# Linear attention into a snake MLP on one core: weights by casting DMAs, filler products, paired PSUM tiles early, and the exponentials of two batches in a row

## The chip, the cores and the metric

The kernel runs on one NeuronCore of a Trainium2 chip. Time is device time in microseconds (us) of one launch on that core; the number that counts is the median of several runs. The engines are PE (TensorE, matrix products), DVE (VectorE), ACT (ScalarE), POOL (GpSimd) and SP (SyncE, which here only starts DMAs). PE's clock has two levels, shown as a granted share of 1.00 or 0.50.

## The reference, cut to what matters

```python
batch, n_heads, seq, head_dim = (8, 8, 576, 64)
n_tokens, d_model, d_ff = (4608, 512, 2048)
...
q_s = q - np.max(q, axis=-1, keepdims=True)
q_s = np.exp(q_s)
q_s = q_s / (np.sum(q_s, axis=-1, keepdims=True) + 1e-09)
k_s = k - np.max(k, axis=2, keepdims=True)
k_s = np.exp(k_s)
k_s = k_s / (np.sum(k_s, axis=2, keepdims=True) + 1e-09)
kv = np.einsum('bhsd,bhse->bhde', k_s, v)
return np.einsum('bhsd,bhde->bhse', q_s, kv).astype(np.float32)
...
x = np.ascontiguousarray(attn_out.transpose(0, 2, 1, 3)).reshape(B * S, H * D)
...
h = x @ w_in
s = np.sin(alpha * h)
g = h + s * s / (alpha + 1e-09)
return (g @ w_out).astype(np.float32)
```

All inputs and the output are float32 in the chip's memory. q, k and v have 9.4 MB each, w_in and w_out 4.19 MB each.

## The kernel before

The work has two halves. **Attention** goes batch by batch (8 of them, called 0 to 7). ACT takes the exponentials of q and k, two instructions each (`exp_q`, `exp_k`); `cast_v` brings v to bfloat16; `norm_q` divides q by its row sums on DVE and POOL. PE then forms k'v (`kv_mm`, 36 products), turns q over (`q_transpose`, 12 products and 6) and multiplies the two (`attn_out`, four groups of 4); between these, DVE or ACT copy each result out of PSUM. The result is `xT`, the tokens of the batch as columns.

The **MLP** goes in 9 tiles t of 512 tokens. For each of 16 slices ni of d_ff, PE makes h (`mm_h`, 4 products of 512 columns), ACT its sine, and then ACT, POOL or DVE squares it (the letter A, P or D of a string such as `SQ0`); DVE adds it up into g (`combine`). Then PE multiplies g by w_out, 64 products of 512 columns for the tile's four groups j of 128 tokens (`mm_o`), and a copy (`evac_o`) goes out by DMA. In this text h(t) and o(t) are these two stages of tile t. Tile t needs batches up to t, so the attention of batch t + 1 is woven into the stages of tile t: the generators `o_pair` and `o_stream` hand out the products of o(t), and `take(os, n)` places n of them between the steps of the attention.

The order on every engine is the order in which the code is written (`tc.manual_schedule()`). Waits come from the buffers: tiles are taken from pools in turn, and a new one waits until the last reader of the buffer is done. PSUM has 8 banks: four for h (`ps_h`), two for o (`ps_o`) and one buffer of two banks for the attention (`ps_a`).

All loads stand on SP's queue, in this order: alpha, q, k and v of batch 0, the four parts of w_in, the four of w_out, then batches 1 and 2. All go through one pool of six float32 buffers (`stage`). The weights are brought to bfloat16 by POOL: w_in part 0 before h(0) starts, the others between the squares of h(0), the last part of w_out after it.

From tile 3 on, the exponentials of batch t + 1 stand behind slice 0 of h(t) (`attn_front`), its matrix products in h(t) (`attn_back`), and o(t - 1) is woven through. Before that, the code is written out: batch 1 in o(0), batch 2 in o(1), batch 3 in h(2), whose slice 2 is followed by the exponentials of batch 3 and by the rest of o(1):

```python
if ni == 2:
    flush(lag, 0)
    attn_front(3, [GP])
    take(os)
attn_back(3, ni - 7)
```

At the start, PE makes 14 products without use (`warm`) while batch 0 is prepared.

Of the kernel before, what the change touches and what calls it, by code (L numbers as in the profile page):

```python
# [23 lines left out]
def kernel(  # L24
# [247 lines left out]

    def cast_win(c, eng, parts=1):
        n = 4 // parts
        for h in range(parts):
            eng(win[:, h * n:(h + 1) * n, c * 512:(c + 1) * 512], wst["i", c][:, h * n:(h + 1) * n])

    def cast_wout(c, eng):
        eng(wout[:, 4 * c:4 * c + 4, :], wst["o", c])  # L279
# [202 lines left out]
```

## Time and profile before

| | |
|---|---|
| median of 3 runs | 320.58 us (320.1 to 322.48) |
| profiled execution, its own time | 321.48 us |
| its span, first to last instruction | 319.7 us |
| PE busy | 290.9 us, 91% of the span |
| ACT, DVE, POOL busy | 231.8, 197.6, 82.8 us |
| mean granted clock of PE | 0.984 |
| DMA, from 3 us to 52 us | about 390 GB/s without a break |

The profiled execution took 1.78 us more than its span, and 0.90 us more than the median. PE is the engine to look at: where it is idle, or at the lower clock, the row just before says what it waited for. From 119 us on the kernel repeats itself every 31.7 us.

### The profile page before, as it was taken

How to read it: one execution, taken by the hardware profiler on the slowest of the kernel's cores; microseconds unless marked ns; L12 is line 12 of the kernel's file. 1: busy time of each engine (PE TensorE's matmuls, PEld its weight loads, DVE VectorE, ACT ScalarE, POOL GpSimd, SP SyncE). 2: the span in 40 equal slices, each digit the busy share in tenths (PEclk: the TensorE clock that was granted, in tenths of full speed). 3: DMA queues.
4: the chain of work that ended last, by engine and by line, in shares of the span. 5: the costliest groups of instructions: out<-in, count | busy, mean ns of one | idle time of the engine just before them, and what ended most of it. 6: DMA issues, size and time to landing. Idle time of an engine off the chain costs nothing.

```text
span 319.7 us, 4552 instructions
## 1 busy us (share of the span) xinstructions
PE 290.9 (91%) x1727; PEld 133.9 (42%) x1727; DVE 197.6 (62%) x281; ACT 231.8 (72%) x321; POOL 82.8 (26%) x58
## 2 busy tenths in 40 slices
PE   2889897999795969999999999999999999999994
PEld 1434343444341524544454445444544444444441
DVE  2738982498535784687568756875687545455511
ACT  4759852997099659976997799779977777777600
POOL 0439970474245550700061007000400000000000
PEclk9959999999998999999999999999999999999999
DMA  7999996780279900111861186111111121111142
GB/s 254 384 387 386 391 391 257 202 309 0 66 225 310 397 23 0 35 36 33 259 252 33 36 264 246 33 33 36 33 35 33 33 56 45 33 33 36 34 98 66
DMA packets 22790, 46.44 MB, mean 145 GB/s; under 512 B 1760, under 2 KB 1776, under 8 KB 22768
## 3 DMA queue, kind: packets, MB, share of 16 engines
q1 hardware_dynamic: 22688, 46.02, 43.9%
q8 instruction: 13, 0.21, 0.3%
q10 hardware_dynamic: 80, 0.13, 0.1%
q14 instruction: 9, 0.07, 0.1%
HBM read 36.71 MB, written 9.44 MB: 144 GB/s over the span
## 4 chain that ended last, share of the span: by engine, by line
PE 54%; ACT 19%; DVE 13%; POOL 7%; issue 4%; DMA 1%; SPq 0%; ACTq 0%; POOLq 0%; DVEq 0%
PE hp L215 23%; PE op L235 23%; DVE g L231 6%; ACT s L221 5%; POOL s L225 3%; ACT qe L119 3%; ACT ke L119 3%; PE tp L185 3%; DVE qs L147 2%; ACT L119 2%; ACT L221 2%; PE xp L198 2%; PE kvp L158 2%; ACT s L223 2%; POOL wout L279 2%
## 5 line engine op out<-in xcount | busy, mean ns | idle before, releaser
L215 PE MATMUL hp<-xT,win 128*128 128x512 bf16 x544 | 140.0, 387 | 8.7 <-DVE g L231 5.9
L231 DVE SCALAR_TENSOR_TENSOR g<-s,inva_sb,hp 128x512 bf16<-128x512 f32 x136 | 100.2, 745 | 70.3 <-ACT s L223 56.1
L235 PE MATMUL op<-wout,g 128*128 128x512 bf16 x544 | 135.5, 379 | 1.7 <-DVE o L244 0.8
L221 ACT ACTIVATE s<-hp,alpha_sb 128x512 f32<-128x512 f32 x136 | 92.2, 683 | 39.2 <-PE hp L215 35.0
L215 PEld LDWEIGHTS <-win 128*128 128x128 bf16 x576 | 56.6, 99 | 79.7 <-issue 16.1
L235 PEld LDWEIGHTS <-g 128*128 128x128 bf16 x576 | 53.5, 98 | 64.6 <-issue 2.3
L223 ACT ACTIVATE s<-s 128x512 f32<-128x512 f32 x115 | 72.4, 630 | 3.7
L149 POOL TENSOR_TENSOR qn<-qe,qs 128x2304 bf16<-128x2304 bf16 (+1 forms) x8 | 26.6, 3328 | 95.3 <-PE hp L215 80.6
L225 POOL TENSOR_TENSOR s<-s 128x512 f32<-128x512 f32 x22 | 25.0, 1144 | 38.4 <-ACT s L221 38.3
L147 DVE TENSOR_REDUCE qs<-qe 128x18 f32<-128x1152 bf16 (+1 forms) x11 | 20.8, 1887 | 17.2 <-ACT qe L119 17.2
L244 DVE COPY o<-op 128x512 f32<-128x512 f32 x32 | 21.5, 674 | 7.1 <-PE op L235 7.1
L201 DVE CAST xT<-xp 128x512 bf16<-128x512 f32 (+1 forms) x26 | 19.1, 739 | 4.4 <-PE xp L198 4.4
L119 ACT ACTIVATE qe<-st_q 128x1152 bf16<-128x1152 f32 x16 | 17.8, 1156 | 4.1 <-DMA st_q<-in_q_dram 4.1
L119 ACT ACTIVATE ke<-st_k 128x1152 bf16<-128x1152 f32 x16 | 17.7, 1150 | 0.7 <-DMA st_k<-in_k_dram 0.7
L133 POOL CAST vb<-st_v 128x1152 bf16<-128x1152 f32 x13 | 15.9, 1252 | 4.2 <-DMA st_v<-in_v_dram 4.2
L201 ACT CAST xT<-xp 128x640 bf16<-128x640 f32 x6 | 4.0, 690 | 15.4 <-PE xp L198 15.4
L198 PE MATMUL xp<-qT,kvb 64*64 64x256 bf16 (+1 forms) x128 | 9.8, 302 | 4.0 <-DVE xT L201 1.2
L185 PE MATMUL tp<-identb,qn 128*128 128x128 bf16 x144 | 10.8, 219 | 3.0 <-ACT qT L186 1.1
L185 PEld LDWEIGHTS <-qn 128*128 128x128 bf16 x144 | 9.1, 98 | 7.6 <-issue 3.9
L198 PEld LDWEIGHTS <-kvb 64*64 64x64 bf16 x128 | 4.7, 103 | 15.8 <-issue 13.9
L158 PE MATMUL kvp<-vb,ke 64*128 64x130 bf16 x288 | 10.3, 223 | 0.7 <-ACT qT L186 0.5
L119 ACT ACT_TABLE_LOAD x8 | 10.3, 1283 | 0.9 <-PEq L466 0.7
(38 smaller groups left out, 113.2 us busy)
## 6 DMA issues: line engine op xcount, KB each, us to landing
out_dram<-o SPq DMA_DIRECT2D x71, 128.0 KB, 2.4
st_q<-in_q_dram SPq DMA_DIRECT2D x7, 1152.0 KB, 5.9
st_k<-in_k_dram SPq DMA_DIRECT2D x7, 1152.0 KB, 8.4
...
st_w<-in_moe_w_out_dram SPq DMA_DIRECT2D x4, 1024.0 KB, 15.4
...
```

The source lines that it names most:

```text
L119: nc.scalar.activation(dst[:, :, ii * 128:(ii + 1) * 128].rearrange("p j (x d) -> p x j d", x=2), src[:, ii::2], AX.Exp)
L147: nc.vector.tensor_reduce(part, src, axis=AXL.X, op=ALU.add)
L149: engs[h].tensor_tensor(dst, src, part.unsqueeze(3).to_broadcast([128, J, w, D]), op=ALU.mult)
L185: nc.tensor.transpose(tp[:, h, 2 * jj + ii], qn[:, j, ii * 128:(ii + 1) * 128], identb)
L201: eng(xT[:, ii::2, c0:c0 + n], xp[:, :, 0:n])
L215: nc.tensor.matmul(hp, win[:, ki, ni * 128:(ni + 1) * 128], xT[:, ki, t * MF:(t + 1) * MF], start=(ki == 0), stop=(ki == 3))
L221: nc.scalar.activation(s, hp, AX.Sin, scale=alpha_sb[:, ni:ni + 1])
L223: nc.scalar.activation(s, s, AX.Square)
L225: nc.gpsimd.tensor_tensor(s, s, s, op=ALU.mult)
L231: nc.vector.scalar_tensor_tensor(G[t][:, ni], in0=s, scalar=inva_sb[:, ni:ni + 1], in1=hp, op0=ALU.mult, op1=ALU.add)
L235: nc.tensor.matmul(acc, G[t][:, ni, j * 128:(j + 1) * 128], wout[:, ni, :], start=(ni == 0), stop=(ni == nN - 1))
L244: eng(o, acc)
```

## The change

The weights no longer pass through float32 buffers and POOL's casts: eight DMAs on POOL's own queue write w_in and w_out to their bfloat16 places, and they stand behind POOL's half of `norm_q(0)`. Batch 1 is loaded from POOL's queue too, after slices 4, 7 and 10 of h(0), and batch 2 after `cast_v(1)`; q and k of batch 3 are loaded before h(1), v of batch 3 after the exponentials of batch 3. `stage` has five buffers in place of six. alpha is loaded by ACT's queue, not ahead of q on SP's.

Four products without use stand before `attn_out` of batch 0 and four behind it. Up to the end of h(1) the four banks of `ps_o` and `ps_a` are one pool of two buffers with two banks each (`ps_e`): a pair of h slices, a pair of o groups, or a step of the attention. h(0) uses the string of h(1), with nine squares on POOL. `qe` has two buffers, and the exponentials of batch 3 follow those of batch 2 on ACT, ahead of o(1); the copies of o(1) stand on ACT behind them. The rest of o(1) is spread over h(2), one product for each slice. A sine of one element (`zero`) loads ACT's table ahead of h(1) and of h(2).

```diff
-    stage = ctx.enter_context(tc.tile_pool(name="stage", bufs=6))
+    stage = ctx.enter_context(tc.tile_pool(name="stage", bufs=5))
...
-    def load(name, t, b, halves=False):
+    def load(name, t, b, halves=False, eng=nc.sync):
...
             for ii in range(2):
-                nc.sync.dma_start(out=flat[:, ii::2], in_=view[:, ii::2])
+                eng.dma_start(out=flat[:, ii::2], in_=view[:, ii::2])
         else:
-            nc.sync.dma_start(out=flat, in_=view)
+            eng.dma_start(out=flat, in_=view)
...
-    wst = {}
-
-    def load_win(c, parts=1):
-        st = stage.tile([128, 4, 512], F32, name="st_w", tag="st")
-        n = 4 // parts
-        for h in range(parts):
-            nc.sync.dma_start(out=st[:, h * n:(h + 1) * n], in_=win_v[:, h * n:(h + 1) * n, c * 512:(c + 1) * 512])
-        wst["i", c] = st
+    def load_win(c):
+        nc.gpsimd.dma_start(out=win[:, :, c * 512:(c + 1) * 512], in_=win_v[:, :, c * 512:(c + 1) * 512])
 
     def load_wout(c):
-        st = stage.tile([128, 4, 512], F32, name="st_w", tag="st")
-        nc.sync.dma_start(out=st, in_=wout_v[:, 4 * c:4 * c + 4, :])
-        wst["o", c] = st
+        nc.gpsimd.dma_start(out=wout[:, 4 * c:4 * c + 4, :], in_=wout_v[:, 4 * c:4 * c + 4, :])
...
     def exp_q(b):
-        A["qe", b] = att1.tile([128, J, 4 * D], BF16, name="qe")
+        A["qe", b] = att2.tile([128, J, 4 * D], BF16, name="qe")
...
         if wide and ni % 6 >= 4:
-            hp = ps_o.tile([128, MF], F32, name="op", tag="o")
+            if ni % 6 == 4:
+                A["hh"] = wide.tile([128, 2, MF], F32, name="hh", tag="a")
+            hp = A["hh"][:, ni % 6 - 4]
         else:
             hp = ps_h.tile([128, MF], F32, name="hp", tag="h")
...
-    nc.sync.dma_start(out=alpha_rows, in_=moe_alpha.rearrange("(no ni) -> no ni", ni=128))
+    nc.scalar.dma_start(out=alpha_rows, in_=moe_alpha.rearrange("(no ni) -> no ni", ni=128))
...
-    load_win(0, parts=2)
-    for c in range(1, 4):
-        load_win(c)
-    for c in range(4):
-        load_wout(c)
-    load("q", q, 1)
-    load("k", k, 1)
-    load("v", v, 1, halves=True)
-    load_batch(2)
...
-        for n in range(14):
-            nc.tensor.matmul(warm, identb, A["qe", 0][:, 0:4, 0:128], start=True, stop=True)
+
+        def warm_up(n):
+            for _ in range(n):
+                nc.tensor.matmul(warm, identb, A["qe", 0][:, 0:4, 0:128], start=True, stop=True)
+
+        warm_up(14)
         norm_q(0, [GP, V])
+        for c in range(4):
+            load_win(c)
+        for c in range(4):
+            load_wout(c)
         cast_v(0, [V, V])
...
         kv_norm(0)
-        cast_win(0, POOL_CP, parts=2)
+        warm_up(4)
         for ii in range(2):
             attn_out(0, ii, 0, ps_s, DVE_CP)
             attn_out(0, ii, 1, ps_s, ACT_CP)
+        warm_up(4)
...
-    ps_o = ctx.enter_context(tc.tile_pool(name="ps_o", bufs=2, space=PSUM, reuse_waits="tile"))
-    ps_a = ctx.enter_context(tc.tile_pool(name="ps_a", bufs=1, space=PSUM, reuse_waits="tile"))
...
-    lag = []
-    SQ0 = "ADPADPADPADPADPA"
-    for ni in range(nN):
-        h_slot(0, ni, SQ0[ni], lag, wide=True)
-        flush(lag, 1)
-        if ni in (0, 2, 5):
-            cast_win((0, 2, 5).index(ni) + 1, POOL_CP)
-        elif ni in (8, 11, 14):
-            cast_wout((8, 11, 14).index(ni), POOL_CP)
-    flush(lag, 0)
-    cast_wout(3, POOL_CP)
...
         for n in range(2):
-            evac_o(t, j0 + n, accs[n], (DVE_CP, ACT_CP)[n])
-            if n == 0:
-                yield
...
+            evac_o(t, j0 + n, accs[n], engs[n])
+        yield
...
-    exp_q(1)
-    norm_q(1, [GP, V])
-    os = o_pair(0, 0, ps_o)
-    take(os)
-    exp_k(1)
-    cast_v(1, [GP, V])
-    os = o_pair(0, 2, ps_h)
-    take(os, 16)
-    q_transpose(1, 0, ps_a, ACT_CP)
-    take(os, 2)
-    q_transpose(1, 1, ps_a, ACT_CP)
-    take(os, 2)
-    kv_mm(1, 0, ps_a)
-    kv_mm(1, 1, ps_a)
-    kv_norm(1)
-    take(os, 6)
-    for ii in range(2):
-        attn_out(1, ii, 0, ps_a, DVE_CP)
...
+    lag = []
+    SQ = "PAPDPAPAPPDPAPAP"
+    with tc.tile_pool(name="ps_e", bufs=2, space=PSUM, reuse_waits="tile") as ps_e:
+        late = {4: ("q", q, 1, False), 7: ("k", k, 1, False), 10: ("v", v, 1, True)}
+        for ni in range(nN):
+            h_slot(0, ni, SQ[ni], lag, ps_e)
+            flush(lag, 1)
+            if ni in late:
+                name, x, b, hv = late[ni]
+                load(name, x, b, halves=hv, eng=GP)
+        flush(lag, 0)
+
+        exp_q(1)
+        norm_q(1, [GP, V])
+        acc = ps_e.tile([128, 2, dm], F32, name="acc", tag="a")
+        take(o_pair(0, 0, [acc[:, 0], acc[:, 1]], [ACT_CP, ACT_CP]))
+        exp_k(1)
+        cast_v(1, [GP, V])
+        for name, x in (("q", q), ("k", k), ("v", v)):
+            load(name, x, 2, eng=GP)
+        os = o_pair(0, 2, [ps_h.tile([128, dm], F32, name="hp", tag="h") for _ in range(2)], [DVE_CP, ACT_CP])
+        take(os, 18)
+        q_transpose(1, 0, ps_e, ACT_CP)
+        nc.scalar.activation(zero, zero, AX.Sin)
         take(os, 2)
-        attn_out(1, ii, 1, ps_a, ACT_CP)
-        take(os, 1)
-    take(os)
-
-    SQ1 = "PAPDPAPAPPDPAPAP"
-    for ni in range(nN):
-        h_slot(1, ni, SQ1[ni], lag, wide=True)
-        flush(lag, 1)
-    flush(lag, 0)
...
+        q_transpose(1, 1, ps_e, DVE_CP)
+        take(os, 2)
+        kv_mm(1, 0, ps_e)
+        kv_mm(1, 1, ps_e)
+        kv_norm(1)
+        take(os, 6)
+        for ii in range(2):
+            attn_out(1, ii, 0, ps_e, DVE_CP)
+            attn_out(1, ii, 1, ps_e, ACT_CP)
+            take(os, 2)
+        take(os)
+        load("q", q, 3)
+        load("k", k, 3)
+
+        for ni in range(nN):
+            h_slot(1, ni, SQ[ni], lag, ps_e)
+            flush(lag, 1)
+            if ni == 14:
+                cast_v(2, [GP, GP])
+        flush(lag, 0)
+
+    ps_o = ctx.enter_context(tc.tile_pool(name="ps_o", bufs=2, space=PSUM, reuse_waits="tile"))
+    ps_a = ctx.enter_context(tc.tile_pool(name="ps_a", bufs=1, space=PSUM, reuse_waits="tile"))
...
+    def o_stream(t, eng=DVE_CP):
...
                 if ni == nN - 1:
-                    evac_o(t, j, acc, DVE_CP, last=(t == nT - 1 and j == 3))
+                    evac_o(t, j, acc, eng, last=(t == nT - 1 and j == 3))
...
-    def attn_front(b, engs):
-        exp_q(b)
-        exp_k(b)
-        cast_v(b, [GP, GP])
-        norm_q(b, engs)
-        if b + 1 < B:
-            load_batch(b + 1)
-
-
-    attn_front(2, [V, GP])
-    os = o_stream(1)
+
+    exp_q(2)
+    exp_k(2)
+    norm_q(2, [V, GP])
+    exp_q(3)
+    exp_k(3)
+    load("v", v, 3)
+    cast_v(3, [GP, GP])
+    nc.scalar.activation(zero, zero, AX.Sin)
+    os = o_stream(1, ACT_CP)
     take(os, 32)
...
-    take(os, 4)
+    take(os, 3)
...
+    norm_q(3, [GP])
     for n in range(4):
-        attn_out(2, n // 2, n % 2, ps_a, (DVE_CP, ACT_CP)[n % 2])
-        take(os, 2)
+        attn_out(2, n // 2, n % 2, ps_a, ACT_CP)
+        take(os, 3)
+    load_batch(4)
...
     for ni in range(nN):
-        hp = h_slot(2, ni, SQ2[ni], lag)
+        h_slot(2, ni, SQ2[ni], lag)
         flush(lag, 1)
-        if ni == 2:
-            flush(lag, 0)
-            attn_front(3, [GP])
-            take(os)
-        attn_back(3, ni - 7)
+        attn_back(3, ni - 6)
+        take(os, 1)
     flush(lag, 0)
+    take(os)
```

On POOL's queue, from its half of the division of q of batch 0 (`qn`) into h(0), before (`st_w` is a float32 buffer of a weight part, L225 a square):

```order
L149 TENSOR_TENSOR qn<-qe,qs 128x9x128
L276 CAST win<-st_w 128x2x512 x2
L276 CAST win<-st_w 128x4x512
L225 TENSOR_TENSOR s<-s 128x512
L276 CAST win<-st_w 128x4x512
L225 TENSOR_TENSOR s<-s 128x512
L276 CAST win<-st_w 128x4x512
L225 TENSOR_TENSOR s<-s 128x512
L279 CAST wout<-st_w 128x2048
```

The same place of POOL's queue in the changed kernel, up to that step of batch 1:

```order
L141 TENSOR_TENSOR qn<-qe,qs 128x9x128
L101 DMA win<-in_moe_w_in_dram 128x4x512 x4
L104 DMA wout<-in_moe_w_out_dram 128x4x512 x4
L219 TENSOR_TENSOR s<-s 128x512 x3
L92 DMA st_q<-in_q_dram 128x4x576
L219 TENSOR_TENSOR s<-s 128x512
L92 DMA st_k<-in_k_dram 128x4x576
L219 TENSOR_TENSOR s<-s 128x512 x2
L90 DMA st_v<-in_v_dram 128x2x576 x2
L219 TENSOR_TENSOR s<-s 128x512 x3
L141 TENSOR_TENSOR qn<-qe,qs 128x9x128
```

Over the whole stretch up to that step of batch 1, nine casts are gone, twelve DMAs have come in, and there are nine squares in place of five.

On ACT's queue, from the last sine of h(1) on, before (`xT` is a copy of the attention of batch 2, L221 a sine of h(2), L223 a square):

```order
L221 ACTIVATE s_761<-hp_756,alpha_sb_87 128x512
L119 ACT_TABLE_LOAD
L119 ACTIVATE qe_766<-st_q_125 128x2x9x64 x2
L119 ACTIVATE ke_769<-st_k_127 128x2x9x64 x2
L201 CAST xT_83<-xp_914 128x2x320
L201 CAST xT_83<-xp_934 128x2x320
L221 ACT_TABLE_LOAD
L221 ACTIVATE s_949<-hp_944,alpha_sb_87 128x512
L221 ACTIVATE s_957<-hp_952,alpha_sb_87 128x512
L223 ACTIVATE s_957<-s_957 128x512
L221 ACTIVATE s_966<-hp_961,alpha_sb_87 128x512
L119 ACT_TABLE_LOAD
```

The exponentials of batch 3 (`qe_971`, `ke_974`) and a second table load follow there. The same place of ACT's queue in the changed kernel (`o<-op` is a copy of a group of o(1)):

```order
L215 ACTIVATE s_750<-hp_745,alpha_sb_87 128x512
L111 ACT_TABLE_LOAD
L111 ACTIVATE qe_762<-st_q_468 128x2x9x64 x2
L111 ACTIVATE ke_765<-st_k_470 128x2x9x64 x2
L111 ACTIVATE qe_776<-st_q_606 128x2x9x64 x2
L111 ACTIVATE ke_779<-st_k_608 128x2x9x64 x2
L384 ACT_TABLE_LOAD
L384 ACTIVATE zero_106<-zero_106 128x1
L238 COPY o_804<-op_787 128x512
L238 COPY o_825<-op_808 128x512
L193 CAST xT_83<-xp_909 128x2x256
```

The exponentials of batch 3 have moved out of h(2) to those of batch 2, one pair of table loads is gone, and the copies of o(1) stand behind all of it.

## Rows read from the trace of the kernel before

**Rows 1.** Windows by stage: h(0) start, attention 1, o(1), h(2) twice, steady tile.

```profile
core 0: us, PE busy (x) PEld busy (x) DVE busy (x) ACT busy (x) POOL busy (x), PEclk, DMA share, GB/s
17.30:23.70 6.40, 6.38 (x17) 2.23 (x17) 2.01 (x3) 2.70 (x4) 2.19 (x2) 0.53 1.05 386
...
46.20:56.50 10.30, 7.76 (x88) 4.11 (x87) 3.38 (x7) 3.01 (x4) 0.00 (x0) 1.00 0.72 265
...
72.40:92.00 19.60, 16.82 (x128) 7.85 (x126) 11.54 (x18) 9.70 (x12) 6.05 (x5) 1.00 0.21 46
92.00:103.00 11.00, 7.11 (x32) 3.00 (x30) 6.38 (x7) 10.88 (x13) 6.86 (x5) 0.94 0.97 339
103.00:119.00 16.00, 12.93 (x107) 6.47 (x106) 12.81 (x21) 9.93 (x16) 8.67 (x9) 0.93 0.59 220
...
151.00:182.70 31.70, 31.33 (x199) 14.51 (x198) 22.01 (x32) 27.30 (x38) 6.32 (x3) 1.00 0.45 146
```

**Rows 2.** Timeline, 0 to 30 us: start, us, engine, line, op, tiles, count.

```profile
1.20 0.92 SPq L90 DMA_DIRECT2D st_q<-in_q_dram  x2
...
8.22 2.13 POOL L149 TENSOR_TENSOR qn<-qe,qs 128x1152 bf16<-128x1152 bf16 x1 [6.91 <-DVE qs L148]
...
11.99 9.11 SPq L111 DMA_DIRECT2D st_w<-in_moe_w_out_dram  x4
...
12.74 0.76 DVE L133 CAST vb<-st_v 128x1152 bf16<-128x1152 f32 x1 [0.51 <-DMA st_v<-in_v_dram]
...
17.32 6.54 PE L215 MATMUL hp<-xT,win 128*128 128x512 bf16 x16 [1.18 <-ACT xT L201]
```

**Rows 3.** One window, the attention products of batch 0 (columns as in rows 1).

```profile
13.00:16.50 3.50, 2.01 (x48) 1.23 (x41) 2.26 (x6) 3.47 (x5) 1.89 (x2) 0.99 1.03 389
```

**Rows 4.** Timeline, 30 to 60 us: batch 1 in o(0), and h(1).

```profile
38.65 2.22 ACT L119 ACTIVATE qe<-st_q 128x1152 bf16<-128x1152 f32 x2 [0.54 <-DMA st_q<-in_q_dram]
...
43.04 1.97 DVE L149 TENSOR_TENSOR qn<-qe,qs 128x1152 bf16<-128x1152 bf16 x1
...
46.46 0.83 PE L185 MATMUL tp<-identb,qn 128*128 128x128 bf16 x12
...
56.54 0.38 PE L215 MATMUL hp<-xT,win 128*128 128x512 bf16 x1
```

**Rows 5.** Waits of PE, 46.2 to 57 us: total, times, longest.

```profile
PE tp L185 <- ACT qT L186: 1.1, 1, 1.1
PE xp L198 <- DVE xT L201: 0.5, 2, 0.3
PE xp L198 <- ACT xT L201: 0.5, 1, 0.5
PE kvp L158 <- ACT qT L186: 0.5, 1, 0.5
```

**Rows 6.** Timeline, 56 to 92 us: batch 2 in o(1), and h(2).

```profile
72.44 1.28 ACT L119 ACT_TABLE_LOAD   x1
...
75.86 2.20 ACT L119 ACTIVATE ke<-st_k 128x1152 bf16<-128x1152 f32 x2
...
80.14 1.02 PE L235 MATMUL op<-wout,g 128*128 128x512 bf16 x4 [0.79 <-DVE o L244]
...
88.89 2.95 PE L215 MATMUL hp<-xT,win 128*128 128x512 bf16 x12
```

**Rows 7.** Timeline, 92 to 135 us: PE in h(2), and the start of tile 3.

```profile
102.21 1.87 PE L215 MATMUL hp<-xT,win 128*128 128x512 bf16 x4 [3.89 <-DVE g L231]
...
118.88 0.81 PE L215 MATMUL hp<-xT,win 128*128 128x512 bf16 x3 [1.22 <-DVE xT L201]
```

**Rows 8.** Chain that ended last, in order of time: its last stretch.

```profile
300.45 14.69 PE op L235 x68
```

**Rows 9.** Timeline, 0 to 60 us: a square on POOL, beside DVE's, and alone.

```profile
29.52 1.48 POOL L225 TENSOR_TENSOR s<-s 128x512 f32<-128x512 f32 x1
...
59.75 1.04 POOL L225 TENSOR_TENSOR s<-s 128x512 f32<-128x512 f32 x1 [13.72 <-ACT s L221]
```

More of the change, by code (lines that the diff above doesn't have):

```diff
@@ L204, with mm_h @@
     G = {}
-    def mm_h(t, ni, wide=False):
+    def mm_h(t, ni, wide=None):
         if ni == 0:
@@ L248, in evac_o @@
             q_eng.dma_start(out=out_v[blk // J, blk % J], in_=o[64 * hf:64 * hf + 64])
-    ACT_CP, DVE_CP, POOL_CP = nc.scalar.copy, nc.vector.tensor_copy, nc.gpsimd.tensor_copy
+    ACT_CP, DVE_CP = nc.scalar.copy, nc.vector.tensor_copy
     V, GP = nc.vector, nc.gpsimd
-    nc.sync.dma_start(out=alpha_rows, in_=moe_alpha.rearrange("(no ni) -> no ni", ni=128))
+    nc.scalar.dma_start(out=alpha_rows, in_=moe_alpha.rearrange("(no ni) -> no ni", ni=128))
     load("q", q, 0, halves=True)
@@ L271 @@
         nc.vector.memset(vb[n].rearrange("p j (i c) -> p j i c", i=4)[:, :, :, D:D + 1], 1.0)
[L273 to L279, printed above, removed]
     with tc.tile_pool(name="ps_s", bufs=4, space=PSUM) as ps_s:
@@ L304, with h_slot @@
             attn_out(0, ii, 1, ps_s, ACT_CP)
+        warm_up(4)
     ps_h = ctx.enter_context(tc.tile_pool(name="ps_h", bufs=4, space=PSUM, reuse_waits="tile"))
-    ps_o = ctx.enter_context(tc.tile_pool(name="ps_o", bufs=2, space=PSUM, reuse_waits="tile"))
-    ps_a = ctx.enter_context(tc.tile_pool(name="ps_a", bufs=1, space=PSUM, reuse_waits="tile"))
-    def h_slot(t, ni, sq, lag, wide=False):
+    def h_slot(t, ni, sq, lag, wide=None):
         hp = mm_h(t, ni, wide)
-        s = sine(t, ni, hp, sq)
-        lag.append((t, ni, hp, s))
-        return lag
+        lag.append((t, ni, hp, sine(t, ni, hp, sq)))
     def flush(lag, keep):
@@ L319, in flush, with o_pair @@
             combine(*lag.pop(0))
-    lag = []
-    SQ0 = "ADPADPADPADPADPA"
-    for ni in range(nN):
-        h_slot(0, ni, SQ0[ni], lag, wide=True)
-        flush(lag, 1)
-        if ni in (0, 2, 5):
-            cast_win((0, 2, 5).index(ni) + 1, POOL_CP)
-        elif ni in (8, 11, 14):
-            cast_wout((8, 11, 14).index(ni), POOL_CP)
-    flush(lag, 0)
-    cast_wout(3, POOL_CP)
-    def o_pair(t, j0, pool):
-        tag = "o" if pool is ps_o else "h"
-        accs = [pool.tile([128, dm], F32, name=tag + "p", tag=tag) for _ in range(2)]
+    def o_pair(t, j0, accs, engs):
         for ni in range(nN):
@@ L340, in o_pair, with take @@
         for n in range(2):
-            evac_o(t, j0 + n, accs[n], (DVE_CP, ACT_CP)[n])
-            if n == 0:
-                yield
-    def take(it, n=None):
-        for _ in iter(int, 1) if n is None else range(n):
+            evac_o(t, j0 + n, accs[n], engs[n])
+        yield
+    def take(it, n=1000):
+        for _ in range(n):
             if next(it, 0) == 0:
                 return
-    exp_q(1)
-    norm_q(1, [GP, V])
-    os = o_pair(0, 0, ps_o)
-    take(os)
-    exp_k(1)
-    cast_v(1, [GP, V])
@@ L444 @@
             if b is not None and ni == 0:
-                attn_front(b, [GP])
+                exp_q(b)
+                exp_k(b)
+                cast_v(b, [GP, GP])
+                norm_q(b, [GP])
+                if b + 1 < B:
+                    load_batch(b + 1)
             want = 20 + 11 * ni // 4 if b is not None else 4 * (ni + 1)
```

3 lines of the change are left out of this document (1 added, 2 removed).

## The prediction

> **What bounds the kernel now.** I read the busy shares by stage first, then the timeline of the stages that are not full, then the DMA's rate in them. From 119 us on PE is full: a tile of 31.7 us has PE busy for 31.33 [rows 1]. That part has the same code after the change, so it can only start sooner or later. A product of 512 columns takes 14.69 / 68 = 0.216 us [rows 8], so 128 of them are 27.65 us, and the attention of one batch is the other 31.33 - 27.65 = 3.7 us.
>
> Before 119 us PE loses time in four places. At the start of h(0) its clock is at the lower level (0.53 granted over 6.4 us) and 16 products take 6.54 us in place of 3.5 [rows 1, 2]: 3.0 us. The attention of batch 1, from its first turning product at 46.46 to h(1) at 56.54, has PE busy for 7.76 of 10.3 us [rows 1, 4]. O(1) has 16.82 of 19.6 us [rows 1]. In h(2) PE is busy for 7.11 of 11.0 and 12.93 of 16.0 us [rows 1]; one wait there is 3.89 us [rows 7], while ACT, busy for 10.88 of 11.0 us, takes exponentials.
>
> The first half has a second bound, which PE's idle time doesn't name. DMA moves 386 to 389 GB/s all through the start [rows 1, 3]; ACT waits 0.54 us for q of batch 1, which lands at 38.65 [rows 4]. Behind it stand exponential, row sums and division, which end at 43.04 + 1.97 = 45.01; PE comes to its turning products at 46.46 [rows 4]. So before the change only 1.4 us lie between what PE could do and what the transfers allow. **Whatever PE gains in h(0) beyond that it waits for again,** unless q of batch 1 lands sooner.
>
> **The change part by part.**
>
> *Transfers.* The same bytes go ahead of q of batch 1: 3.54 MB of batch 0, 8.39 MB of weights, 1.18 MB of q. Alpha no longer stands ahead of q on SP, whose first load starts at 1.20 us [rows 2]; I take 0.46 us of that back for all of batch 0. Then v of batch 0 lands at 12.74 - 0.46 = 12.3 [rows 2]. The weights can start only when POOL's half of the division is done, at 8.22 + 2.13 - 0.46 = 9.9 [rows 2]. A first part of 1.05 MB at 389 GB/s takes 2.7 us. The trace shows no DMA from POOL's queue and none that casts. From below I take SP's way, where weights queue up without a gap: then q lands at 38.65 - 0.46 = 38.2. From above I take 2.3 us of idle DMA, as long as SP was held for one weight DMA (9.11 us for four) [rows 2]. I take a gap of 1.1, the middle, since nothing is queued behind batch 0 until POOL has issued: q of batch 1 at 39.3, 0.65 later than before, and the division at 45.7. For the rate I take 389 GB/s as read, because the bytes read are the same; the ends are under the rivals.
>
> *Fillers.* In the window before the clock fell PE was busy for 2.01 of 3.5 us [rows 3]; between the products of batch 1 it was busy for 75% and the clock stayed at 1.00 [rows 1]. Eight fillers of 0.216 us put the former at over 80%, so I take it that the clock holds: 3.0 us less in h(0). Four of them are 0.86 us in a gap of that length ahead of `attn_out`; the other four lie in the wait for xT of 1.18 us [rows 2]. H(0) then starts at 17.3 at the latest, and with 64 * 0.216 = 13.8 plus 0.4 ends at 31.5. The 32 products of the first pair and 18 of the second end at 42.3. But the division ends at 45.7: **PE waits 3.4 us there, so the fillers' gain ends in this wait,** and POOL's casts, now gone, free it for nine squares without moving the end either. If the clock falls all the same, h(0) ends 3.0 later, still ahead of 45.7: price nothing.
>
> *Paired PSUM tiles.* From the first turning product to h(1) it was 10.08 us [rows 4]. Two more products are done before (0.43). Of PE's waits for a copy in this stretch, 1.1 + 0.5 + 0.5 + 0.5 us [rows 5], two buffers leave about 0.5. So 10.08 - 0.43 - 2.1 = 7.55, and h(1) starts at 45.7 + 7.55 = 53.2 in place of 56.54: **3.3 us sooner.** The copies of the first o pair now stand on ACT between the exponentials of q and k; k lands 3 us behind q, which hides them.
>
> *H(1) and o(1).* The table load of the exponentials came 72.44 - 56.54 = 15.9 us after the start of h(1) [rows 4, 6]; with the sine's table loaded ahead I take 15.4, so 68.6. Then ACT has one table load (1.28), four times two exponentials (2.2 each) [rows 6], the second load (1.28), 0.2 for `zero`, and only then the first copy of o(1), 0.6 and 0.1 to be seen: 12.3 us, to 80.9. PE has its 32 products and k'v done about 4 us sooner, and waits for that copy: it goes on at 81.0, against 80.14 before [rows 6]. **Here the gain of 3.3 us is gone and 0.9 with it.** `cast_v(2)` ahead of POOL's last square falls into the same wait. From there to h(2) it was 88.89 - 80.14 = 8.75 us [rows 6]; three more products make it 9.4. A wait of 3.89 us was followed by four products in 1.87 us, double their time [rows 7], and this wait is as long, so I add 1.0 for the clock: h(2) at 91.4.
>
> *H(2).* Before, from its start to that of tile 3 it was 118.88 - 88.89 = 29.99 us [rows 6, 7], with the exponentials inside. Now it has 64 products and the 11 that are left of o(1), 75 * 0.216 = 16.2, and one attention, 3.7: 19.9, and 0.7 for copies that PE waits for. ACT has some 17 us of work in it and is no longer the bound. Tile 3 starts at 91.4 + 20.6 = 112.0 in place of 118.88: **6.9 us sooner.** Batch 4 is loaded at about 91 us, long before its exponentials. Five buffers in place of six cost nothing, since a batch's three tiles come free during the exponentials that stand ahead of the next loads.
>
> **The sum.** Span 319.7 - 6.9 = 312.8; with the 1.78 around it 314.6 for the profiled execution; that lay 0.90 above the median, so **313.7 us**, 2.1% less.
>
> **Rivals.**
>
> *The casting transfers are slower (on the slower side).* Each us by which q of batch 1 lands later moves everything behind it by one. The weights take 21.6 us at 389 GB/s; with 28.5, at 294 GB/s, the whole gain is gone, and at 250 GB/s (33.6 us) the time is 325.7. At half the rate it would be 335. For it: no row shows such a transfer. Against: the same bytes leave the memory, and fewer are written. Chance 0.14.
>
> *POOL is held by issuing.* Squares stand behind eight DMAs on POOL, four more lie between them. SP was held for 9.11 us by four weight DMAs, 2.3 each, with its queue full [rows 2]. At c us for each, the weights are issued at 9.9 + 8c; nine squares of about 1.26 [rows 9] and four more DMAs follow, so h(0) ends at 21.2 + 12c and batch 1's products can come 10.8 later. Up to c = 1.14 that is hidden by the wait for q; at 1.7 the gain of 6.9 us is gone; at 2.3 it is 7 us more, 321 to 328. I take 318.5 for it, with chance 0.21.
>
> *DVE holds up POOL's DMAs.* A square on POOL takes 1.04 us alone and 1.48 beside DVE's work [rows 9], so the two engines get in each other's way; and in the weights' first 3 us DVE casts v, 0.76 us twice [rows 2]. If both casts stop POOL, q lands 1.5 us later: 315.2. The Trainium skill, "SBUF — State Buffer", section "SBUF: two separate sides", has this as a trap: descriptors of a DMA issued by GpSimd are written by its cores, and a copy in VectorE's two-port mode locks them out, so that the transfer looks blocked. By that rule the later time holds; the row shows such slowing between two computing operations, and no run here shows it for a DMA. The chance of this rival is 0.10.
>
> *The transfers are faster.* If fewer bytes written let the weights run a tenth faster, q lands 2.0 us sooner, PE still waits for it, and the time is 311.7, or 310.7 if the wait in o(1) costs no clock. Chance 0.10.
>
> **How the numbers follow.** The forecast has 0.45, with a range of its own from 311.5 to 316.5 (a gap of 0 to 2.3 us, the clock in o(1) kept or lost). A run of this kernel tells 1% (3.2 us) from no change, so faster ends at 317.4. Faster: the forecast, DVE's hold (0.10), the faster transfers (0.10) and 0.02 of the issuing rival, 0.67. Same: 0.13 of the issuing rival and 0.06 of the slow transfers (those at 260 to 320 GB/s), 0.19. Slower: their other 0.06 and 0.08. The range takes in all but the slow ends of these two and what lies below the faster case: 310 to 322.
>
> **What would show it.** The profile after should have: h(0) at a clock of 1.00; PE idle for 3 us before the turning products of batch 1, with q of batch 1 landing at about 39; h(1) at 53; PE idle for about 4 us in o(1), ended by ACT's copy; h(2) in about 20.6 us without a wait of 3.9; tile 3 at 112. It is wrong if q of batch 1 lands after 44, if POOL's first square starts after 22, or if h(2) takes over 25 us.

## The result, and the profile after

The changed kernel takes 313.06 us in the median of four runs (312.41 to 313.86), the kernel before 321.53 beside it (320.1 to 322.66). The ratio is 0.974, with a 95% interval from 0.9683 to 0.9796. A second set of runs gave 313.66 against 321.56, ratio 0.9749 [0.9724, 0.9775]. The profiled execution took 313.65 us with a span of 311.8, against 321.48 and 319.7.

The page of the kernel after first: busy time by engine, the queue that POOL feeds, the weights' issues (KB each, median us from issue to landing), and from the costliest groups one with a new name, `hh`, for the h slices in a paired tile.

```profile
PE 288.6 (93%) x1735; PEld 134.0 (43%) x1735; DVE 192.4 (62%) x272; ACT 231.6 (74%) x326; POOL 81.9 (26%) x68
...
q0 software_dynamic: 5872, 11.27, 14.5%
...
win<-in_moe_w_in_dram POOLq DMA_DIRECT2D x4, 512.0 KB, 8.6
wout<-in_moe_w_out_dram POOLq DMA_DIRECT2D x4, 512.0 KB, 16.3
...
L209 PE MATMUL hh<-xT,win 128*128 128x512 bf16 x32 | 8.2, 378 | 3.1 <-ACT s L215 3.1
```

PE is busy for 93% of the span. The weights land 8.6 (w_in) and 16.3 us (w_out) after their issue in the median. PE's idle time ahead of `hh` is 3.1 us, all of it ended by a sine on ACT.

The same stages as in [rows 1], as windows of the kernel after, with the first transfers of the weights ahead of them:

```profile
core 0: us, PE busy (x) PEld busy (x) DVE busy (x) ACT busy (x) POOL busy (x), PEclk, DMA share, GB/s
11.50:12.00 0.50, 0.50 (x13) 0.50 (x10) 0.50 (x1) 0.10 (x1) 0.50 (x1) 1.00 1.00 86
12.00:12.50 0.50, 0.50 (x18) 0.40 (x17) 0.07 (x2) 0.50 (x1) 0.50 (x2) 1.00 0.55 55
17.30:23.70 6.40, 5.62 (x28) 2.44 (x26) 3.28 (x5) 3.86 (x7) 3.12 (x3) 1.00 1.24 206
43.84:50.93 7.09, 6.55 (x86) 3.58 (x84) 4.67 (x8) 3.95 (x5) 3.68 (x4) 1.00 0.68 221
66.80:80.00 13.20, 8.38 (x69) 4.07 (x68) 7.62 (x11) 13.12 (x16) 7.73 (x7) 1.00 0.27 89
82.00:84.00 2.00, 2.00 (x12) 1.16 (x10) 0.96 (x1) 0.00 (x0) 0.00 (x0) 0.50 0.75 170
88.74:110.40 21.66, 20.30 (x147) 9.82 (x146) 14.73 (x23) 14.90 (x24) 10.75 (x9) 1.00 0.72 239
142.90:174.60 31.70, 31.33 (x200) 14.49 (x198) 22.08 (x31) 27.25 (x38) 6.31 (x3) 1.00 0.45 146
```

The steady tile is what it was: 31.33 of 31.7 us on PE. The start of h(0) has its clock at 1.00 in place of 0.53. While the weights come, the column on the right reads 206 GB/s. It counts what is written: POOL's queue is listed with 11.27 MB, which is 4.19 MB of weights as bfloat16 and 7.08 MB of batches 1 and 2, and both pages list the same 36.71 MB read from memory. Each bfloat16 byte written is two float32 bytes read, so 412 GB/s are read where the trace before had 386 [rows 1]. The attention of batch 1 has PE busy for 6.55 of 7.09 us, before 7.76 of 10.3. O(1) got worse in its first part: PE is busy for 8.38 of 13.2 us, where before it was busy for 8.37 of the 9.38 us from the start of o(1) at 70.76 to 80.14. H(2) is nearly full: 20.30 of 21.66.

The timeline from 0 to 30 us shows POOL's issues, the fillers (`warm`), and PE in h(0):

```profile
9.74 3.75 POOL L101 DMA_DIRECT2D win<-in_moe_w_in_dram  x4
...
13.49 2.97 POOL L104 DMA_DIRECT2D wout<-in_moe_w_out_dram  x4
...
13.87 1.04 PE L271 MATMUL warm<-qe,identb 128*128 128x512 bf16 x4
...
17.36 3.62 PE L209 MATMUL hp<-xT,win 128*128 128x512 bf16 x16
...
19.20 1.03 POOL L219 TENSOR_TENSOR s<-s 128x512 f32<-128x512 f32 x1 [2.74 <-ACT s L215]
...
22.62 1.02 PE L209 MATMUL hh<-xT,win 128*128 128x512 bf16 x4 [0.78 <-ACT s L215]
```

Sixteen products take 3.62 us where they took 6.54 [rows 2]. POOL has issued everything at 16.46 and then waits 2.74 us for work. The last row is a wait that the kernel before doesn't have. From 30 to 60 us, with the steps of batch 1 that [rows 4] shows of before:

```profile
33.05 7.07 PE L229 MATMUL acc<-wout,g 128*128 128x512 bf16 x32
...
37.72 2.22 ACT L111 ACTIVATE qe<-st_q 128x1152 bf16<-128x1152 f32 x2 [2.02 <-DMA st_q<-in_q_dram]
...
42.12 1.97 DVE L141 TENSOR_TENSOR qn<-qe,qs 128x1152 bf16<-128x1152 bf16 x1
...
43.84 1.09 PE L177 MATMUL tp<-identb,qn 128*128 128x128 bf16 x12
...
50.93 3.81 PE L209 MATMUL hp<-xT,win 128*128 128x512 bf16 x16
```

The exponentials of q start 0.9 us sooner than before, the turning products 2.6 and h(1) 5.6 sooner. Then o(1) and the start of h(2), to be held against [rows 6]:

```profile
66.81 3.40 PE L229 MATMUL op<-wout,g 128*128 128x512 bf16 x15
...
68.18 1.28 ACT L111 ACT_TABLE_LOAD   x1
...
79.42 1.05 ACT L238 COPY o<-op 128x512 f32<-128x512 f32 x2
...
80.03 0.81 PE L229 MATMUL op<-wout,g 128*128 128x512 bf16 x3 [3.56 <-ACT o L238]
...
88.74 1.03 PE L209 MATMUL hp<-xT,win 128*128 128x512 bf16 x4
```

PE waits 3.56 us in o(1) for a copy that stands on ACT behind all exponentials of batches 2 and 3 (ACT is busy for 11.82 of the 11.85 us from the table load to 80.03), and it goes on at 80.03, before at 80.14 [rows 6]: at this point nothing of the 5.6 us is left. H(2) starts where it started before, 88.74 against 88.89 [rows 6]. The whole gain comes out of h(2) after that. The end of h(2) in the timeline from 92 to 125 us:

```profile
109.51 2.07 PE L209 MATMUL hp<-xT,win 128*128 128x512 bf16 x8
...
111.42 4.48 PE L229 MATMUL op<-wout,g 128*128 128x512 bf16 x20
```

The last four of the eight products at 109.51 are the first of tile 3, so it starts at 110.4; before, its second product came at 118.88, behind a wait for `xT` [rows 7]. O(2) starts at 111.42, before at 119.53, 8.1 us sooner, and the span is 7.9 us shorter.

### The profile page after: what moved, and what is told of

The parts are those of the page before. It is cut to its first block, busy times and chain, and to the rows that moved or that the text cites. A ratio compares the mean times of both kernels' runs of the same rounds, so it can differ in the third digit from the quotient of the medians.

```text
span 311.8 us, 4560 instructions
## 1 busy us (share of the span) xinstructions
PE 288.6 (93%) x1735; PEld 134.0 (43%) x1735; DVE 192.4 (62%) x272; ACT 231.6 (74%) x326; POOL 81.9 (26%) x68
## 3 DMA queue, kind: packets, MB, share of 16 engines
q1 hardware_dynamic: 15232, 30.55, 31.7%
q0 software_dynamic: 5872, 11.27, 14.5%
HBM read 36.71 MB, written 9.44 MB: 148 GB/s over the span
## 4 chain that ended last, share of the span: by engine, by line
PE 60%; ACT 18%; DMA 7%; DVE 6%; issue 4%; POOL 3%; SPq 1%; ACTq 0%
PE hp L209 27%; PE op L229 24%; ACT s L215 5%; DMA st_q<-in_q_dram 4%; ACT ke L111 4%; ACT qe L111 3%; DVE g L225 3%; DMA st_v<-in_v_dram 3%; PE kvp L150 2%; PE tp L177 2%; ACT L111 2%; PE xp L190 2%; ACT s L217 2%; ACT L215 2%; PE hh L209 2%
## 5 line engine op out<-in xcount | busy, mean ns | idle before, releaser
L225 DVE SCALAR_TENSOR_TENSOR g<-s,inva_sb,hp 128x512 bf16<-128x512 f32 x136 | 100.4, 746 | 73.8 <-ACT s L217 54.9
L209 PE MATMUL hp<-xT,win 128*128 128x512 bf16 x544 | 136.9, 379 | 2.2 <-DVE g L225 2.1
L229 PE MATMUL op<-wout,g 128*128 128x512 bf16 x512 | 130.5, 381 | 4.9 <-ACT o L238 3.6
L219 POOL TENSOR_TENSOR s<-s 128x512 f32<-128x512 f32 x26 | 27.1, 1045 | 29.2 <-ACT s L215 29.1
L139 DVE TENSOR_REDUCE qs<-qe 128x18 f32<-128x1152 bf16 (+1 forms) x11 | 20.7, 1886 | 15.4 <-ACT qe L111 15.3
L238 DVE COPY o<-op 128x512 f32<-128x512 f32 x27 | 18.3, 676 | 7.1 <-PE op L229 7.1
L193 DVE CAST xT<-xp 128x512 bf16<-128x512 f32 (+1 forms) x24 | 17.7, 742 | 1.3 <-PE xp L190 1.3
L178 DVE COPY qT<-tp 128x768 bf16<-128x768 bf16 (+1 forms) x13 | 9.6, 736 | 5.5 <-PE tp L177 5.5
L177 PE MATMUL tp<-identb,qn 128*128 128x128 bf16 x144 | 11.8, 231 | 0.5 <-DVE qn L141 0.4
L177 PEld LDWEIGHTS <-qn 128*128 128x128 bf16 x144 | 10.0, 104 | 4.8 <-issue 1.4
L193 ACT CAST xT<-xp 128x640 bf16<-128x640 f32 (+1 forms) x8 | 5.3, 665 | 7.8 <-PE xp L190 7.7
L209 PE MATMUL hh<-xT,win 128*128 128x512 bf16 x32 | 8.2, 378 | 3.1 <-ACT s L215 3.1
## 6 DMA issues: line engine op xcount, KB each, us to landing
wout<-in_moe_w_out_dram POOLq DMA_DIRECT2D x4, 512.0 KB, 16.3
```

Of the source, the lines that this page charges most:

```text
L139: nc.vector.tensor_reduce(part, src, axis=AXL.X, op=ALU.add)
L177: nc.tensor.transpose(tp[:, h, 2 * jj + ii], qn[:, j, ii * 128:(ii + 1) * 128], identb)
L193: eng(xT[:, ii::2, c0:c0 + n], xp[:, :, 0:n])
L209: nc.tensor.matmul(hp, win[:, ki, ni * 128:(ni + 1) * 128], xT[:, ki, t * MF:(t + 1) * MF], start=(ki == 0), stop=(ki == 3))
L219: nc.gpsimd.tensor_tensor(s, s, s, op=ALU.mult)
L225: nc.vector.scalar_tensor_tensor(G[t][:, ni], in0=s, scalar=inva_sb[:, ni:ni + 1], in1=hp, op0=ALU.mult, op1=ALU.add)
```

## The experiments

The runs came in three sets, each beside the kernel before, whose median was 321.56, 321.26 and 320.83 us in them. A difference "to the kernel after" is one of medians, with its second set of runs (313.66, beside 321.56). For a kernel of the second or third set up to 0.3 or 0.7 us of it can come from the set.

**Is the fillers' gain eaten by the wait for q?** My theory: yes, PE waits for the division anyway. The rival: the clock's loss goes on to the end. This experiment leaves the fillers out; each of the next two moves one end of the wait that the theory names.

```diff
-        warm_up(4)
...
-        warm_up(4)
```

> Both groups of four fillers are left out. Theory of the forecast: PE's clock falls in h(0), h(0) ends 3 us later, but PE waits for q of batch 1 anyway, so the time stays at 313. Rival, from the trace after: PE reached the turning products of batch 1 at 43.84 us and the division ended at 44.09, so there is no wait left, and the fillers are worth what they save: 2.5 to 3 us more, about 316, with PE's clock at 0.5 in h(0).

314.86 us (314.09 to 316.74), ratio 0.9802 [0.9771, 0.9833], 1.2 more than the kernel after; all six runs lie above all eight of the kernel after. In the profiled run the clock fell; the same window as above, of this kernel (PE alone):

```profile
17.30:23.70 6.40, 6.13 (x16) 0.56 1.24 202
```

The start of the turning products in this kernel's timeline, and the starts of these and of h(1) in the profile of the kernel after from the same set:

```profile
46.57 0.83 PE L177 MATMUL tp<-identb,qn 128*128 128x128 bf16 x12
...
43.78 0.83 PE L177 MATMUL tp<-identb,qn 128*128 128x128 bf16 x12
...
50.61 1.66 PE L209 MATMUL hp<-xT,win 128*128 128x512 bf16 x6
```

The turning products start 2.8 us later than in that profile, and h(1) and h(2) at 53.40 and 92.13 are later by 2.8 and 2.5, and the spans differ by 2.8 (315.0 against 312.2): nothing of the loss is hidden. That run took 316.74 us with a mean granted clock of 0.975, and one other has the same numbers (316.69 at 0.976); the remaining four took 314.1 to 315.1 with clocks from 0.985 to 0.994. So the fillers bring some 3 us in an execution whose clock falls there. That the other four kept their clock in h(0), and so lost only about 1 us, is not shown: they have no trace. The theory falls: the wait of 3.4 us that was to hide this isn't there.

**Is q of batch 1 what PE waits for?** One POOL issue moves: q of batch 1 between w_in and w_out.

```diff
         for c in range(4):
             load_win(c)
+        load("q", q, 1, eng=GP)
...
-        late = {4: ("q", q, 1, False), 7: ("k", k, 1, False), 10: ("v", v, 1, True)}
+        late = {7: ("k", k, 1, False), 10: ("v", v, 1, True)}
```

> q of batch 1 is loaded from POOL's queue between w_in and w_out, not after slice 4 of h(0); it lands some 9 us sooner, and w_out 3 us later, still before its use. Theory of the forecast: PE waits for this load, so the stage gets up to 3 us shorter, 310.5. Rival, from the trace after: PE comes to the turning products when the division ends (43.84 and 44.09 us), so the load is no longer what sets the time: 313.2 to 313.7, as the changed kernel.

313.76 us (312.28 to 313.97), ratio 0.976 [0.9735, 0.9785]: no change. Its timeline shows why:

```profile
35.83 2.22 ACT L111 ACTIVATE qe<-st_q 128x1152 bf16<-128x1152 f32 x2
...
40.08 4.05 PE L229 MATMUL hp<-wout,g 128*128 128x512 bf16 x17
...
40.23 1.96 DVE L141 TENSOR_TENSOR qn<-qe,qs 128x1152 bf16<-128x1152 bf16 x1
...
43.96 0.83 PE L177 MATMUL tp<-identb,qn 128*128 128x128 bf16 x12
```

The exponentials start 1.9 us sooner and wait for no transfer, the division ends at 42.2, and PE comes to it at 43.96 as before, since it still has o(0)'s products to do. PE is the bound there.

**What made h(0) longer than its products?** Each h slice of a pair gets a tile of its own (two banks, one used), so that the second needn't wait for the sine of the first. The number of buffers stays.

```diff
-            if ni % 6 == 4:
-                A["hh"] = wide.tile([128, 2, MF], F32, name="hh", tag="a")
-            hp = A["hh"][:, ni % 6 - 4]
+            hp = wide.tile([128, 2, MF], F32, name="hh", tag="a")[:, 0]
```

> Slices 4, 5, 10 and 11 of h(0) and h(1) take a two-bank buffer each, of which they use one bank, in place of sharing one; the number of buffers at work is as before. Theory of the forecast: pairs of h slices cost nothing, 313. Rival: the second slice of a pair waits 0.78 us for the sine of the first, four times; h(0) gets 1.5 us shorter, and PE then waits for q of batch 1 instead (no gain there, 0.2 at most); h(1) gets 1.5 us shorter, of which ACT's sines let 1.0 to 1.5 through: 311.5 to 312.

311.77 us (310.66 to 312.24), ratio 0.9688 [0.966, 0.9716], 1.9 less than the kernel after. The four waits of 0.78 us are gone from PE's waits. H(0) takes 13.82 us in place of 15.69, h(1) 14.00 in place of 15.88. But in the first of the two stages the gain turns into another wait, as the timeline shows:

```profile
31.22 7.07 PE L227 MATMUL acc<-wout,g 128*128 128x512 bf16 x32
...
37.52 2.22 ACT L111 ACTIVATE qe<-st_q 128x1152 bf16<-128x1152 f32 x2 [3.53 <-DMA st_q<-in_q_dram]
...
42.72 0.23 PE L177 MATMUL tp<-identb,qn 128*128 128x128 bf16 x1 [0.55 <-POOL qn L141]
...
43.94 0.79 PE L177 MATMUL tp<-identb,qn 128*128 128x128 bf16 x11 [0.99 <-DVE qn L141]
```

Now PE waits 0.55 and 0.99 us for both halves of the division: the wait that the prediction had, 1.5 us of it, in a kernel whose h(0) is as short as the prediction had it. H(1) starts at 50.73, no sooner than the 50.61 of the kernel after: the 1.9 us at the end are those of h(1).

**What is the wait in o(1) worth?** DVE makes the copies of o(1) in place of ACT.

```diff
-    os = o_stream(1, ACT_CP)
+    os = o_stream(1, DVE_CP)
```

> The copies of o(1) are made by DVE in place of ACT, so that they don't stand behind the exponentials of batch 3. Theory: these copies hold PE for 3.56 us in o(1), and the clock that falls in that wait costs another 1 us; PE is then held by the division of q of batch 2 on POOL (78.3 us in the trace after, in place of the copy at 80.0), so 2.5 to 3.5 us go: 309.5 to 310.5. Rival: the exponentials of batch 3 on ACT and DVE's work set the end of this stage anyway, through the copies of the attention on ACT and the row sums on DVE: less than 1 us, 312 to 313.

310.38 us (310.22 to 311.12), ratio 0.9656 [0.963, 0.9681], 3.3 less than the kernel after. Its timeline in o(1):

```profile
75.86 1.22 DVE L238 COPY o<-op 128x512 f32<-128x512 f32 x2
...
76.54 0.81 PE L229 MATMUL op<-wout,g 128*128 128x512 bf16 x2
```

The window from 80 to 92 us of this kernel, PE alone:

```profile
80.00:92.00 12.00, 11.17 (x65) 1.00 0.51 161
```

The same window of the kernel after, in its second profile:

```profile
80.00:92.00 12.00, 11.59 (x65) 0.77 0.33 71
```

PE goes on 3.2 us sooner (76.54 against 79.72 in that second profile), and the clock doesn't fall behind it. From 76 to 92 us the granted clock is 0.79 to 0.89 in all six traces of the changed kernel and its variants that have this wait, and 1.00 in the four without it. The wait went through to the end; after it PE waits 0.79 us for `kvb` on DVE, not for the division on POOL that I had expected. The 3.3 us hold both the wait and the clock: the three runs of the kernel after with a mean clock of 0.999 (312.41, 312.47 and 313.05 us) lie only 2.0 to 2.7 above this kernel's median.

**What do the exponentials in a row bring?** Those of batch 3, with the cast of v, the division, the loads of batch 4 and the rest of o(1), go back behind slice 2 of h(2), as in the kernel before.

```diff
-    exp_q(3)
-    exp_k(3)
...
-    cast_v(3, [GP, GP])
...
-    norm_q(3, [GP])
...
-    load_batch(4)
...
-        attn_back(3, ni - 6)
-        take(os, 1)
+        if ni == 2:
+            flush(lag, 0)
+            exp_q(3)
+            exp_k(3)
+            cast_v(3, [GP, GP])
+            norm_q(3, [GP])
+            load_batch(4)
+            take(os)
+        attn_back(3, ni - 7)
```

> The exponentials, cast and division of batch 3 go back behind slice 2 of h(2), followed by the rest of o(1), as before the change; all else is as after. Theory of the forecast: of 6.9 us the exponentials together bring about 3.6 net, so 316.5 to 318; h(2) has its wait of 3.9 us again, and o(1) loses its wait for ACT's copy. Rival: the move only carries PE's wait from h(2) to o(1), and the gain is all in the first 51 us: 313 to 314.

317.9 us (317.81 to 318.47), ratio 0.9904 [0.9882, 0.9926], 4.2 more. PE goes on in o(1) at 76.68 without a wait for the copy and reaches h(2) at 85.59, 3 us sooner than the kernel after; then the old wait is back, and the four products behind it take 1.82 us, against 1.03 at the full clock:

```profile
85.59 2.75 PE L209 MATMUL hp<-xT,win 128*128 128x512 bf16 x12
...
99.04 1.82 PE L209 MATMUL hp<-xT,win 128*128 128x512 bf16 x4 [4.87 <-DVE g L225]
...
115.92 4.48 PE L229 MATMUL op<-wout,g 128*128 128x512 bf16 x20
```

O(2) starts at 115.92 in place of 111.42. So the step brings over 7 us inside h(2) and gives 3 of them back in o(1) ahead of it.

**What does the second PSUM pair bring?** A tile with two small products holds one of the two attention buffers from batch 1's turning products to h(1), so only one is left, as before.

```diff
+        hold = ps_e.tile([128, 2, dm], F32, name="hold", tag="a")
+        nc.tensor.matmul(hold[:, 0, 0:128], identb, identb, start=True, stop=True)
...
+        nc.tensor.matmul(hold[:, 0, 0:128], identb, identb, start=True, stop=True)
```

> The changed kernel with one of the two buffers of the early PSUM pool held by two small products from the first to the last step of batch 1's attention, so that these steps have one buffer, as before the change. Theory: two buffers save the waits for copies, 2.1 us or more: 315.7 to 317. Rival: the order of the steps brought it, and the buffers nothing: 313.7.

318.52 us (317.52 to 319.03), ratio 0.9922 [0.9898, 0.9946], 4.9 more, or 5.6 when each is held against the kernel before beside it. From the first turning product to h(1) it takes 10.70 us, in place of 6.83 in that second profile of the kernel after. The timeline shows PE waiting for the copy that frees the one buffer, twice of several:

```profile
46.33 0.49 PE L177 MATMUL tp<-identb,qn 128*128 128x128 bf16 x6 [1.10 <-ACT qT L178]
...
53.32 0.48 PE L190 MATMUL xp<-qT,kvb 64*64 64x320 bf16 x4 [0.79 <-DVE xT L193]
```

The window of that stage (columns as in the first windows), and one across its end (PE alone), which shows that the clock fell as well:

```profile
43.97:54.67 10.70, 7.54 (x88) 3.92 (x86) 4.82 (x8) 4.31 (x5) 3.34 (x4) 0.92 0.82 290
...
53.40:56.80 3.40, 3.40 (x13) 0.55 0.99 355
```

**Parts alone, in the kernel before.** One kernel has only the casting weight DMAs, with POOL's casts gone and the later loads on POOL; one has only the eight fillers.

```diff
-        nc.sync.dma_start(out=st, in_=wout_v[:, 4 * c:4 * c + 4, :])
...
+        nc.gpsimd.dma_start(out=win[:, :, c * 512:(c + 1) * 512], in_=win_v[:, :, c * 512:(c + 1) * 512])
...
-        if ni in (0, 2, 5):
-            cast_win((0, 2, 5).index(ni) + 1, POOL_CP)
```

> The kernel before, with one part of the change: weights by casting DMAs on POOL's queue behind its division, batch 1 and 2 loaded from POOL's queue at the places of the changed kernel, no casts on POOL. Theory: the load of q of batch 1 and the casts between POOL's squares set the pace of the start, so about 1 us goes (q lands 1 us sooner, PE comes to the turning products at 45.4): 320.5. Rival: POOL's casts held the whole of h(0), and 2.5 us or more go: 319 or less.

319.59 us over 12 runs, ratio 0.9959 [0.994, 0.9977]: 1.7 us less than before, between what the theory and its rival had said. Two windows of its profile:

```profile
17.30:23.70 6.40, 5.78 (x27) 2.62 (x28) 2.81 (x5) 5.14 (x9) 1.80 (x2) 1.00 1.24 206
46.00:50.00 4.00, 3.47 (x44) 2.48 (x45) 0.00 (x0) 1.22 (x2) 1.53 (x3) 0.57 0.88 257
```

In this execution the clock held in h(0) without a filler, and o(0) began at 31.68 in place of 34.95. Then PE waited for the division of batch 1, and the clock fell behind that, at 46: of 3.3 us 1.4 reached h(1).

```diff
+        for n in range(4):
+            nc.tensor.matmul(warm, identb, A["qe", 0][:, 0:4, 0:128], start=True, stop=True)
```

The four products stand at both places, ahead of `attn_out` and behind it.

> The kernel before, with the eight fillers alone. Theory: the clock holds in h(0), but the casts of w_in on POOL and the load of q of batch 1 (division at 45.0 us, PE at 46.46) let at most 1.4 us of it through: 320.2 to 321.5. Rival: the clock is worth its 3 us wherever it is saved: 318.5.

320.52 us over 12 runs, ratio 0.9985 [0.9967, 1.0003]: no more than the noise. In the profiled run the clock held in h(0) and o(0) began 2.0 us sooner, h(1) 1.35 sooner. The runs spread from 319.87 us at a mean clock of 0.999 to 321.76 at 0.986.

**Better than both.** DVE's copies in o(1) and the h slices apart, together; and the same with q of batch 1 early.

> As the run with three edits, but q of batch 1 loaded where the changed kernel loads it. Theory: PE waits 1.5 to 1.9 us for the division of batch 1 again, so 308 to 309, above the run with three. Rival: no difference from the run with three.

308.69 us (307.86 to 310.26), ratio 0.9631 [0.9601, 0.9661]. In its trace PE waits 1.1 and 1.0 us for the division of batch 1.

> The changed kernel with three edits: h slices in buffers of their own, copies of o(1) on DVE, q of batch 1 loaded ahead of w_out. Theory: the load, idle as a bound by itself, sets the start once h(0) is 1.9 us shorter; with all three, h(0) 1.9, h(1) 1.9 and o(1) 3.2 us go: 306.5 to 307.5. Rival: the edits give only what each gave alone (2.0, 3.1 and 0): 308.5.

307.16 us (306.9 to 307.6), ratio 0.9573 [0.955, 0.9595]: 6.5 us less than the kernel after, or 5.8 when each is held against the kernel before beside it. The load order that changed nothing in the kernel after is worth 1.5 us here in the medians (0.8 between the two profiles, where h(1) starts at 50.15 and 50.99), since h(0) is short enough for q to matter. The timeline shows the next bound, w_out, which now lands last:

```profile
35.10 1.89 PE L227 MATMUL acc<-wout,g 128*128 128x512 bf16 x8 [0.40 <-DMA wout<-in_moe_w_out_dram]
...
37.71 1.89 PE L227 MATMUL acc<-wout,g 128*128 128x512 bf16 x8 [0.72 <-DMA wout<-in_moe_w_out_dram]
...
43.32 0.83 PE L177 MATMUL tp<-identb,qn 128*128 128x128 bf16 x12
```

## Why the prediction was right, and where it wasn't

The forecast was 313.7 us, 2.1% less than the 320.58 known then; measured were 313.06 beside 321.53, 2.6% less. Its large terms hold; steps between them were wrong and cancelled. Its steps against the profile after (us from the span's start):

| step | before | forecast | after |
|---|---|---|---|
| first weight issue on POOL | | 9.9 | 9.74 |
| h(0) starts | 17.32 | 17.3 | 17.36 |
| o(0) starts | 34.95 | 31.5 | 33.05 |
| exponentials of q, batch 1 | 38.65 | 39.3 | 37.72 |
| division ends | 45.01 | 45.7 | 44.09 |
| first turning product | 46.46 | 45.7 | 43.84 |
| h(1) | 56.54 | 53.2 | 50.93 |
| table load in o(1) | 72.44 | 68.6 | 68.18 |
| PE goes on in o(1) | 80.14 | 81.0 | 80.03 |
| h(2) | 88.89 | 91.4 | 88.74 |
| tile 3 | 118.88 | 112.0 | 110.4 |

**The transfers** were mis-sized to the safe side. From v of batch 0 (DVE's second cast of it starts at 12.43) to q of batch 1 (37.72) it took 25.3 us, forecast 27.0 (12.3 to 39.3). The idle stretch was at most 1.0 us (11.5 to 12.5, at 86 and 55 GB/s) against 1.1 taken. At 412 GB/s read the 8.39 MB of weights need 20.4 us in place of the 21.6 at 389; at the mean from 13 to 32 us, 201 GB/s written and 402 read, it is 20.9. So gap and rate account for 0.8 to 1.3 of the 1.7 us, and the rest stays open. That is the rival of the faster transfers, with a rate 3 to 6% higher rather than a tenth. The slow one, which I gave 0.14, has nothing for it. POOL was not held by issuing: eight DMAs took 6.72 us, 0.84 each, which is under the 1.14 from which it was to count. SP's 2.3 us, the upper end of that rival, was a mean: three of its four weight DMAs took 2.4 to 2.8 us and the last 0.81, and that a full queue held it is not shown.

**DVE's hold on POOL's DMAs** stayed small. The four issues of w_in, during which DVE casts v for 1.04 and 0.76 us, took 3.75 us, the four of w_out without such a cast 2.97: 0.8 us of holding at most, and POOL had 2.74 us to spare behind it. The first of the two casts took 0.75 us in the kernel before and 1.04 here, so DVE was slower as well. The Trainium skill, "SBUF — State Buffer", section "SBUF: two separate sides", has the loser of the shared port blocked for the whole instruction; by that rule up to 1.8 us could go, and this trace shows less than half of it. Whether part of the idle stretch from 11.5 to 12.5 us is such a hold isn't shown.

**The failed step is the fillers',** "PE waits 3.4 us there, so the fillers' gain ends in this wait", with its "price nothing" for a fallen clock. In the profile after, PE's weight loads wait 0.4 us for the division at that place, and its twelve turning products take 1.09 us in place of 0.83; in the second profile of that kernel nothing waits there. Two sizes made the difference: o(0) began 1.55 us later than forecast, and the division ended 1.6 sooner; 3.4 less these is 0.25. The first is the h slices in pairs. I had costed the paired tiles only as attention buffers; that the two slices of a pair share one tile, and that the second waits 0.78 us for the sine of the first, wasn't in the sum. It happens twice in h(0) and twice in h(1), and the run with the slices apart shows what it costs: 1.9 us in each stage. That run also brings part of the forecast's wait back, so the mechanism was right and its two sides stood closer together than I had them.

**The attention of batch 1** took 7.09 us from its first turning product, 7.55 forecast. The experiment with one buffer puts 3.9 us on the second pair in that stage, where I had 2.1 of waits and a total of 2.5. The trace of that run lists 3.2 us of waits in the stage in place of 0.3, so 2.9 of the 3.9 are waits, more than [rows 5] let expect. The other 1.0 is longer busy time, with a mean granted clock of 0.92 in the stage. About 0.7 us of the 4.9 at the end is the clock that fell in h(1) in that run.

**H(1)** has the pairs too: the table load came 17.25 us after its start, 15.4 forecast. H(1) had started 2.3 us ahead of the forecast, so the table load came at 68.18, near the forecast by two errors against each other. **O(1)** went as said: ACT's chain of table load, eight exponentials, table load and copy is what PE waits for, and the wait of 3.56 us takes back all that was won. The 1.0 us for the clock behind it fits two runs of four: 313.65 and 313.86 us with a mean clock of 0.991, against 312.41 and 312.47 with 0.999; only the first of them has a trace, with a clock of 0.50 from 82 to 84 us. From there to h(2) it took 8.71 us rather than 10.4, because I had added three products and the clock to a stretch that had idle time for them: before, PE waited 1.7 us in it for other engines, and after no wait is listed there.

**H(2)** with tile 3 behind it took 21.6 us, forecast 20.6, before 29.99. This is the term that carries the result, and putting the exponentials back costs 4.2 us, the 7 within h(2) less the 3 in o(1).

**Luck** has a part in the closeness. The span was forecast at 312.8 us and was 311.8. The 0.90 us taken off between the profiled execution and the median was the distance of one execution: the two profiled ones of the kernel after lay 0.59 and 0.28 above their medians, and that of the kernel before 0.05 below the median of its four runs.

What stays open: how much of the fillers' worth belongs to each of the two places, and in what share of executions the clock falls without them. What the casting DMAs bring in the kernel after was not tried, nor were the nine squares on POOL, the early table loads and the load of alpha by themselves. The three parts that were taken back (1.2, 4.2 and 4.9 us) come to more than the 7.9 us of the whole change, so their worths overlap and can't be added.
